# Second MLP's first layer: seven products of halves for eight

## The chip, the cores and the metric

One core of a Trainium2 chip runs the kernel. The metric is the device time of one execution in microseconds (us). TensorE multiplies into PSUM banks; VectorE (DVE), ScalarE (ACT) and GpSimd (POOL) work on tiles in SBUF, and VectorE and ScalarE also read PSUM; the DMA queue of SyncE (SP) moves tiles between SBUF and DRAM.

## The reference

Landmark attention over q, k, v of shape (4, 8, 576, 64) gives 2304 tokens of 512 numbers; a gated MLP with 1536 hidden units follows, and then the second MLP with 2048 hidden units, which the change is about:

```python
def _moe2_ref(x, w_in, w_out, alpha):          # x: 2304 x 512
    h = x @ w_in                               # w_in: 512 x 2048
    g = np.maximum(h, 0.0) + alpha * np.minimum(h, 0.0)
    return (g @ w_out).astype(np.float32)      # w_out: 2048 x 512
```

Weights arrive in float64, all else in float32.

## The kernel before

**Arithmetic.** Every large product is made in three terms. `split` (L113) cuts a float32 tile into a high half (ScalarE casts it to the matmul's type) and a low half (VectorE, or POOL where `lo="pool"`, subtracts), and a product is high x low + low x high + high x high (`TERMS`, L57). So a product of 128 x 512 by 512 x n costs 3 x 4 matmuls of n columns.

**First MLP** (L750 to 808). 96 steps, `at` = 24 b + i, each of 12 matmuls of 288 columns in `layer1` (L638) and 12 in `layer2` (L657), which runs two steps behind. Attention of later batches, the folding of weights (`fold`, `take`, `store_folded`, `take_stored`) and the float64 to float32 conversion of the second MLP's weights (`narrow_w2`, from step 36, one tile in 1.4 steps, stored to DRAM as `w2d`) are placed between the steps by tables of step numbers. Its output is stored to DRAM as `x2d`, one tile for 288 tokens.

**Second MLP** (L812 to 908). Tokens go in blocks of 512 (the last has 256). `load_x2` reads a block of `x2d` and splits it, POOL making the low halves. All 32 weight tiles (16 of `w_in`, 16 of `w_out`) are read from `w2d`, split by `convert_w2` and kept in SBUF, the first from step 56 on, most from step 85. For each block and each of the 16 tiles f of hidden units, `layer3` makes 12 matmuls into one bank (tag `gv`, two banks), two VectorE instructions apply the activation, and `split` makes the halves. `layer4` then adds 3 matmuls of 512 columns for each 128 tokens into that token tile's bank (tags `acc` and `att`, six banks); it runs two f behind (`LAG2`, L901):

```python
        behind2.append((i, f, layer3(xs[i], blocks[i][1], f)))
        if behind:
            catch_up()
        if len(behind2) > LAG2:
            catch_up2()
```

**Order.** The program is written once; a scheduler then orders each engine's instructions when the kernel is built, keeping to what each needs and, where several could go, to the order of writing. On the chip each engine works through its own list in order: an instruction that waits holds up all that stand behind it on its engine. Tiles of a tag share its buffers, and a new tile waits until an old one is read. Tag `ws` has 27 buffers of 128 x 1024 float32, the store for weights of both MLPs.

Of the kernel before, what the change touches and what calls it, by code (L numbers as in the profile page):

```python
# [9 lines left out]
F32 = mybir.dt.float32  # L10
F32R = mybir.dt.float32r
# [4 lines left out]
ALU = mybir.AluOpType  # L16
# [5 lines left out]
def tile_landmark_attention_glu_prelu(  # L22
# [66 lines left out]

    w2d = [dpool.tile([P, NW], F32, name=f"w2d{i}", tag=f"w2d{i}") for i in range(2 * NF2)]  # L90
# [603 lines left out]
    def convert_w2(i):  # L694
        t = rpool.tile([P, NW], F32, tag="st2", name="st2", bufs=2)
        nc.sync.dma_start(out=t, in_=w2d[i])
        split(w2_slot(i), t)
# [6 lines left out]
    nc.vector.tensor_copy(alphaT, pa[:, :NF2])  # L704

# [13 lines left out]
    w2_todo, to_narrow = deque(range(2 * NF2)), deque(range(2 * NF2))  # L719
    narrow_pace = 0.0  # L720
    qpool = rpool = None
# [5 lines left out]
    def catch_up():  # L727
# [8 lines left out]
        for m in range(NK):  # L736
# [4 lines left out]
            if f1 == NF1:  # L741
                to = bpool.tile([P, HB], F32, tag="xs", name="xs", bufs=XS_BUFS)
# [7 lines left out]
    for b in range(B):  # L750
# [5 lines left out]
        for i, (half, f, f0, f1) in enumerate(order):  # L756
# [45 lines left out]
            if qpool is not None and at > FOLD_AT[2][-1]:  # L802
                if at % W2_EVERY == 0:
                    if w2_todo and w2_todo[0] < W2_EARLY:
                        convert_w2(w2_todo.popleft())
                if at >= W2_FROM:
                    if w2_todo:
                        convert_w2(w2_todo.popleft())

    blocks = [(n0, min(512, NT - n0)) for n0 in range(0, NT, 512)]  # L812

    def load_x2(n0, n):
        pool = q2pool if n0 // 512 % 2 else qpool
        xs = pool.tile([P, 2, NK, 512], F32R, tag="x2", name="x2", bufs=1)
        for kk in range(NK):
            xr = qpool.tile([P, 512], F32, tag="xr", name="xr", bufs=2)
            done = 0
            while done < n:  # L820
                bl, o = divmod(n0 + done, HB)
                step = min(n - done, HB - o)
                nc.sync.dma_start(out=xr[:, done : done + step], in_=x2d[bl][:, kk, o : o + step])
                done += step
            split(xs[:, :, kk, :n], xr[:, :n], lo="pool")
        return xs

    def layer3(xs, n, f):
        ps = bank("h", "gv")
        w = w2_in[f].rearrange("p a (k c) -> p a k c", k=NK)  # L830
        i = 0
        for a, e in TERMS:
            for kk in range(NK):
                nc.tensor.matmul(  # L834
                    ps[:, :n], lhsT=w[:, a, kk], rhs=xs[:, e, kk, :n], start=(i == 0), stop=(i == 11)
                )
                i += 1
        g = qpool.tile([P, 512], F32, tag="g2", name="g2", bufs=2)
        gs = bpool.tile([P, 2, 512], F32R, tag="A", name="g2s", bufs=4)
        nc.vector.tensor_scalar(  # L840
            out=g[:, :n], in0=ps[:, :n], scalar1=0.0, scalar2=alphaT[:, f : f + 1],
            op0=ALU.min, op1=ALU.mult,
        )
        nc.vector.scalar_tensor_tensor(  # L844
            out=g[:, :n], in0=ps[:, :n], scalar=0.0, in1=g[:, :n], op0=ALU.max, op1=ALU.add
        )
        split(gs[:, :, :n], g[:, :n])
        return gs

    def layer4(acc, gs, f, t):  # L850
        for i, (a, e) in enumerate(TERMS):
            nc.tensor.matmul(  # L852
                acc,
                lhsT=gs[:, a, P * t : P * t + P],
                rhs=w2_out[f][:, e, :],
                start=(f == 0 and i == 0),
                stop=(f == NF2 - 1 and i == 2),
            )
# [13 lines left out]

    order = [(i, f) for i in range(len(blocks)) for f in range(NF2)]
    xs = {0: load_x2(*blocks[0])}
    accs2, behind2 = {}, deque()
    w2_pace = 0.0

    def catch_up2():
        i, f, gs = behind2.popleft()
        n0, n = blocks[i]  # L880
        if f == 0:
            accs2[i] = [
                bank(f"o{t}", ("acc", "att", "acc")[(2 * i + t // 2) % 3]) for t in range(n // P)
            ]
        for t in range(n // P):
            layer4(accs2[i][t], gs, f, t)
            if f == NF2 - 1:
                store(accs2[i][t], n0 + t * P, t)

    for i, f in order:  # L890
        if i == 0 and f == X2_AT[0]:
            while w2_todo:
                convert_w2(w2_todo.popleft())
            rpool.release()
            q2pool = ctx.enter_context(tc.tile_pool(name="q2pool", bufs=1, reuse_waits="tile"))
        if f == X2_AT[i > 0] and i + 1 < len(blocks):
            xs[i + 1] = load_x2(*blocks[i + 1])
        behind2.append((i, f, layer3(xs[i], blocks[i][1], f)))
        if behind:
            catch_up()  # L900
        if len(behind2) > LAG2:  # L901
            catch_up2()
        w2_pace += W2_STEP
        while w2_todo and w2_pace >= 1:
            w2_pace -= 1
            convert_w2(w2_todo.popleft())
    while behind2:
        catch_up2()
# [30 lines left out]
```

## Time and profile before

| | us |
|---|---|
| median of 3 runs | 900.9 (900.38 to 901.02) |
| profiled execution | 904.5 |
| its span | 902.7 |
| first MLP and attention, until the first matmul of layer 3 | 500.5 |
| second MLP, first to last matmul | 397 |

The profile is of one execution, which took 904.5 us, 1.8 us of it outside the span. Busy time of an engine counts the instructions that compute; TensorE's weight loads (PEld) are a row of their own and run beside its matmuls. A matmul's record is longer than its share of TensorE's time, because matmuls overlap; the time from the start of one group to the start of the next is what a group costs.

### The profile page before, as it was taken

The page shows a single profiled execution, that of the slowest core. Times are in us where ns is not written, and L with a number is a line of the kernel's source. Part 1 is how long each engine was busy: PE and PEld are TensorE (multiplying, and loading weights), DVE is VectorE, ACT ScalarE, POOL GpSimd, SP SyncE. Part 2 cuts the span into 40 slices and gives each one's busy share as a digit, 9 for nine tenths or more (in the row PEclk, how much of TensorE's full clock was granted, in tenths as well). Part 3 has the DMA queues.
Part 4 walks back from the last instruction along what each step waited for, and adds up shares of the span by engine and source line. Part 5 has one row for each costly group of instructions (what it writes and reads, how often), then busy time and mean ns, then how long its engine had stood idle before and what let it go on. Part 6 is the DMA issues. An engine that isn't in the chain of part 4 may idle for free.

```text
span 902.7 us, 15122 instructions
## 1 busy us (share of the span) xinstructions
PE 855.3 (95%) x5969; PEld 712.0 (79%) x5969; DVE 506.6 (56%) x1005; ACT 337.2 (37%) x711; POOL 92.4 (10%) x90
## 2 busy tenths in 40 slices
PE   5689889899999999998999999999999999999997
PEld 4367667676887877998999888888888888888896
DVE  3788988577756344676745654443444433444443
ACT  6666865465654233465535421121121111111111
POOL 0131112110111000134100020110010001000000
PEclk9679999989999999999999999999999999999999
DMA  9676778969612152687824520030012000100100
GB/s 263 229 228 174 252 237 242 274 227 248 185 45 85 48 170 90 221 297 230 258 78 129 145 70 1 4 90 1 1 24 58 1 1 13 48 0 1 29 20 24
DMA packets 85160, 106.92 MB, mean 118 GB/s; under 512 B 35664, under 2 KB 57184, under 8 KB 85088
## 3 DMA queue, kind: packets, MB, share of 16 engines
q1 hardware_dynamic: 81632, 93.36, 34.3%
q0 software_dynamic: 3456, 12.58, 4.5%
q8 instruction: 47, 0.77, 0.4%
q14 instruction: 25, 0.20, 0.1%
HBM read 78.65 MB, written 27.26 MB: 117 GB/s over the span
## 4 chain that ended last, share of the span: by engine, by line
PE 82%; DMA 7%; DVE 4%; ACT 3%; issue 2%; SPq 1%; POOL 1%; DVEq 0%; ACTq 0%
PE h L834 22%; PE o L852 22%; PE gv L638 15%; PE acc L657 13%; PE psf L600 3%; DMA raw<-in_moe_w_in_dram 2%; PE psq L191 2%; DMA raw<-in_moe_w_out_dram 1%; DMA w2d<-n 1%; DVE raw L139 1%; PE psz L403 1%; PE psv L314 1%; DMA tk<-in_k_dram 1%; PE psa L210 1%; PE psc L210 1%
## 5 line engine op out<-in xcount | busy, mean ns | idle before, releaser
L638 PE MATMUL gv<-A,we 128*128 128x288 f32 x1152 | 198.8, 313 | 6.6 <-ACT g L649 4.1
L638 PEld LDWEIGHTS gv<-A,we 128*128 128x128 f32 x1152 | 167.7, 196 | 37.6 <-issue 24.7
L657 PE MATMUL acc<-gs,wconv 128*128 128x288 f32 x1152 | 184.4, 303 | 6.9 <-DVE gs L116 4.7
L834 PE MATMUL h<-x,w 128*128 128x512 f32 (+1 forms) x840 | 183.7, 368 | 0.0
L657 PEld LDWEIGHTS acc<-gs,wconv 128*128 128x128 f32 x1152 | 163.9, 192 | 18.6 <-issue 9.3
L852 PE MATMUL o<-w,g2s 128*128 128x512 f32 x702 | 170.0, 389 | 0.0
L834 PEld LDWEIGHTS h<-x,w 128*128 128x128 f32 x840 | 148.0, 188 | 27.2
L852 PEld LDWEIGHTS o<-w,g2s 128*128 128x128 f32 x702 | 131.0, 188 | 26.6
L115 ACT CAST g2s<-g 128x512 fp32r<-128x512 f32 (+1 forms) x80 | 46.4, 580 | 277.0 <-DVE g L844 277.0
L840 DVE TENSOR_SCALAR g<-h,alphaT 128x512 f32<-128x512 f32 (+1 forms) x80 | 55.8, 697 | 155.7 <-PE h L834 155.7
L116 DVE TENSOR_TENSOR g2s<-g,g2s 128x512 fp32r<-128x512 f32 (+1 forms) x80 | 55.9, 699 | 54.6 <-ACT g2s L115 54.0
L116 DVE TENSOR_TENSOR gs<-g,gs 128x288 fp32r<-128x288 f32 x96 | 52.8, 550 | 25.6 <-ACT gs L115 25.2
L650 DVE TENSOR_TENSOR g<-g,gv 128x288 f32<-128x288 f32 x96 | 43.1, 449 | 39.7 <-PE gv L638 35.9
L649 ACT ACTIVATE g<-gv 128x288 f32<-128x288 f32 x96 | 39.4, 411 | 54.6 <-PE gv L638 53.3
L130 ACT ACTIVATE raw<-raw 128x512 f32<-128x512 f32 x68 | 46.7, 687 | 34.8 <-DMA raw<-in_moe_w_in_dram 17.8
L115 ACT CAST gs<-g 128x288 fp32r<-128x288 f32 x96 | 41.6, 433 | 45.6 <-DVE g L650 45.2
L116 POOL TENSOR_TENSOR x<-xr,x 128x512 fp32r<-128x512 f32 (+1 forms) x20 | 24.2, 1219 | 315.3 <-ACT x L115 313.3
L139 DVE SCALAR_TENSOR_TENSOR raw<-raw 128x512 uint32<-128x512 uint32 x68 | 50.1, 748 | 7.4 <-ACT raw L134 6.3
L844 DVE SCALAR_TENSOR_TENSOR g<-h,g 128x512 f32<-128x512 f32 (+1 forms) x80 | 51.0, 638 | 2.7
L600 PE MATMUL psf<-wgv,m 64*32 64x512 f32 x384 | 42.3, 620 | 0.9 <-DVE wgv L142 0.5
L116 DVE TENSOR_TENSOR we<-psf,we 128x512 fp32r<-128x512 f32 x36 | 23.5, 684 | 13.1 <-ACT we L115 13.1
L142 DVE SCALAR_TENSOR_TENSOR n<-raw 128x512 uint32<-128x512 uint32 x32 | 24.8, 775 | 9.6 <-DMA w2d<-n 9.5
(129 smaller groups left out, 728.2 us busy)
## 6 DMA issues: line engine op xcount, KB each, us to landing
raw<-in_moe_w_out_dram SPq DMA_DIRECT2D x28, 512.0 KB, 5.4
wgv<-wgvd POOLq DMA_DIRECT2D x24, 512.0 KB, 4.9
raw<-in_moe_w_in_dram SPq DMA_DIRECT2D x16, 512.0 KB, 4.8
w2d<-n SPq DMA_DIRECT2D x32, 256.0 KB, 2.8
st<-w2d SPq DMA_DIRECT2D x32, 256.0 KB, 2.7
raw<-in_moe_w_gate_dram SPq DMA_DIRECT2D x24, 256.0 KB, 4.5
raw<-in_moe_w_val_dram SPq DMA_DIRECT2D x24, 256.0 KB, 4.8
wgvd<-wgv SPq DMA_DIRECT2D x12, 512.0 KB, 6.2
```

What stands on the lines that cost most here:

```text
L115: nc.scalar.copy(dst[:, 0, :], src)
L116: (nc.gpsimd if lo == "pool" else nc.vector).tensor_tensor(out=dst[:, 1, :], in0=src, in1=f32(dst[:, 0, :]), op=ALU.subtract)
L130: nc.scalar.activation(w[:, :, 1], w[:, :, 1], AF.Copy, scale=2.0 ** -112)
L139: nc.vector.scalar_tensor_tensor(out=lo, in0=hi, scalar=0x80000000, in1=lo, op0=ALU.bitwise_and, op1=ALU.bitwise_or)
L600: nc.tensor.matmul(pss[j][LM * h : LM * h + LM], lhsT=att[b, j, "M"][d, u], rhs=wgv[c, j][d, u], start=True, stop=True,)
L638: nc.tensor.matmul(ps[:, :HB], lhsT=We[b, c, j][:, a, 256 * i + P * s : 256 * i + P * s + P], rhs=att[b, j, "A"][half][:, e, :], start=(n ...
L650: nc.vector.tensor_tensor(out=g, in0=g, in1=pss[1][:, :HB], op=ALU.mult)
L657: nc.tensor.matmul(acc[m][:, :HB], lhsT=wout_sb[f][:, a, P * m : P * m + P], rhs=gs[:, e, :], start=(f == f0 and n == 0), stop=(f == f1 - ...
L834: nc.tensor.matmul(ps[:, :n], lhsT=w[:, a, kk], rhs=xs[:, e, kk, :n], start=(i == 0), stop=(i == 11))
L840: nc.vector.tensor_scalar(out=g[:, :n], in0=ps[:, :n], scalar1=0.0, scalar2=alphaT[:, f : f + 1], op0=ALU.min, op1=ALU.mult,)
L844: nc.vector.scalar_tensor_tensor(out=g[:, :n], in0=ps[:, :n], scalar=0.0, in1=g[:, :n], op0=ALU.max, op1=ALU.add)
L852: nc.tensor.matmul(acc, lhsT=gs[:, a, P * t : P * t + P], rhs=w2_out[f][:, e, :], start=(f == 0 and i == 0), stop=(f == NF2 - 1 and i == 2),)
```

## The change

The first layer of the second MLP is made by Strassen's scheme (in the form with seven products and shared sums). The hidden tiles 2g and 2g + 1, the contraction's halves (256 each) and two halves of a group of 768 tokens make a 2 x 2 product of blocks: a11, a12, a21, a22 from `w_in`, b11, b12, b21, b22 from x, eight products of blocks, each 6 matmuls of 384 columns. Seven products of sums of blocks take their place, and their results are added up to h11 (tile 2g, first half of the tokens), h12, h21 and h22.

- There are 3 groups of tokens and 8 pairs of hidden tiles, 24 calls of `pair`. A product has its bank (tag `gv`, two of them) until it is read: product 1 by a ScalarE copy, the others by `plus`, a VectorE addition of a bank to a tile (7 in a pair; product 5 is read by two).
- Sums of weights (4 VectorE instructions of 128 x 256) and the halves of all seven left operands are made in `make_w7`, during group 0 only, a pair or two ahead, and stored to DRAM (`w7d`); groups 1 and 2 load them (`load_w7`, four DMAs a pair).
- Sums of x and their halves (14 tiles of 128 x 2 x 384) are made in `make_x7`: for group 0 at steps 74 and 83 of the first MLP, on ScalarE and VectorE; for the others during the last pair of the group before, half of the low parts on POOL. There are 15 buffers for 14 tiles, so a new one waits until a product of the last pair has been made.
- The activation is two Relus on ScalarE and one VectorE scale-and-add (`activated`).
- Layer 4 follows in `catch_up2`, three matmuls at a time, 12 calls a pair, and is no longer held back by a lag. `convert_w2`, `w2_slot` and `load_x2` are gone; `w_out` is split in `make_w2_out`, pair by pair, in group 0.
- The narrowed weights' tile `n2` has one buffer throughout; it had two in the later part of the first MLP.

```diff
-    W2_OWN, W2_RAW = (0, 1), (29, 30, 31)
-    W2_EARLY, W2_EVERY = 4, 2
-    W2_FROM, W2_STEP, X2_AT = 85, 3, (11, 6)
+    NG, HG = 3, 384
+    X2_AT, W2_AT = (74, 83), (88, 91)
+    X2_LOAD, X2_SPLIT = 6, 7
...
-            st = qpool.tile([P, NW], F32, tag="xr", name="st3", bufs=2)
+            st = rpool.tile([P, NW], F32, tag="st3", name="st3", bufs=2)
...
+    ORDER7 = (1, 2, 6, 7, 5, 4, 3)
+    PLACE7 = {1: (0, 0), 2: (0, 1), 6: (1, 0), 5: (1, 1), 7: (2, 0), 3: (2, 1), 4: (3, 0)}
...
+    def make_w7(g):
+        n = ws_tile("n7", (P, 2, NW), F32)
+        for i in range(2):
+            nc.sync.dma_start(out=n[:, i], in_=w2d[2 * (2 * g + i)])
+        a11, a12 = n[:, 0, :256], n[:, 0, 256:]
+        a21, a22 = n[:, 1, :256], n[:, 1, 256:]
+        s = ws_tile("s7", (P, 4, 256), F32)
+        for o, x, y, op in (
+            (1, a21, a22, ALU.add),
+            (0, s[:, 1], a11, ALU.subtract),
+            (2, a11, a21, ALU.subtract),
+            (3, a12, s[:, 0], ALU.subtract),
+        ):
+            nc.vector.tensor_tensor(out=s[:, o], in0=x, in1=y, op=op)
+        w7[g] = [ws_tile("w7") for _ in range(4)]
+        split2(w7[g][0], n[:, 0].rearrange("p (o c) -> p o c", o=2))
+        split2(w7[g][1], s[:, 0:2])
+        split2(w7[g][2], s[:, 2:4])
+        split2(w7[g][3][:, 0:1], n[:, 1:2, 256:])
+        for i in range(4):
+            m = 2 if i < 3 else 1
+            nc.sync.dma_start(out=w7d[g][i][:, :m], in_=f32(w7[g][i][:, :m]))
...
-        t = pool.tile([P, NW], F32, tag="n2", name="n2", bufs=1 if rpool is None else 2)
+        t = pool.tile([P, NW], F32, tag="n2", name="n2", bufs=1)
...
+    def make_x7(i, ops):
+        b11, b12, b21, b22, t2 = (xf[i][n] for n in ((0, 0), (0, 1), (1, 0), (1, 1), "T2"))
...
+            for kk in range(2):
+                t = home([P, 2, HG], F32R, "x7")
+                x7[i, op, kk] = t
+                split(t, src[:, kk], lo="pool" if i > 0 and kk else "dve")
...
+    def product(i, g, op):
+        ps = bank("prod", "gv")
+        place, o = PLACE7[op]
+        w = w7[g][place][:, o].rearrange("p (a k c) -> p a k c", a=2, k=2)
+        n = 0
+        for a, e in TERMS:
+            for kk in range(2):
+                nc.tensor.matmul(
+                    ps[:, :HG], lhsT=w[:, a, kk], rhs=x7[i, op, kk][:, e],
+                    start=(n == 0), stop=(n == 5),
+                )
+                n += 1
+        return ps[:, :HG]
...
+    def activated(h, f):
+        n = half("n", "gs")
+        nc.scalar.activation(n, h, AF.Relu, scale=-1.0)
+        nc.scalar.activation(h, h, AF.Relu)
+        nc.vector.scalar_tensor_tensor(
+            out=h, in0=n, scalar=minus_alpha[:, f : f + 1], in1=h, op0=ALU.mult, op1=ALU.add
+        )
...
+        split(gs, h)
+        return gs
...
+    def pair(i, g):
+        f = 2 * g
+        ps = product(i, g, 1)
+        p1 = half("p1")
+        nc.scalar.copy(p1, ps)
+        h11 = plus(p1, product(i, g, 2), "h11", "gs")
+        ready(i, f, 0, activated(h11, f))
+        catch_up2(1)
+        u2 = plus(p1, product(i, g, 6), "u2")
+        catch_up2(1)
+        u3 = plus(u2, product(i, g, 7), "u3")
+        catch_up2(1)
+        ps = product(i, g, 5)
+        h22 = plus(u3, ps, "h22", "gs")
+        u4 = plus(u2, ps, "u4")
+        ready(i, f + 1, 1, activated(h22, f + 1))
+        catch_up2(2)
+        h21 = plus(u3, product(i, g, 4), "h21", "gs")
+        ready(i, f + 1, 0, activated(h21, f + 1))
+        catch_up2(2)
+        h12 = plus(u4, product(i, g, 3), "h12", "gs")
+        ready(i, f, 1, activated(h12, f))
+        catch_up2(5)
```

The order of instructions on TensorE in the second MLP before, in the second block of tokens (h is layer 3's bank, o0 to o3 the banks of four token tiles, w2 weights, g2s activated halves):

```order
L834 MATMUL h_6845<-x2_6291,w2_6509 128x512 x12
L852 MATMUL o0_6435<-w2_6463,g2s_6797 128x512 x3
L852 MATMUL o1_6436<-w2_6463,g2s_6797 128x512 x3
L852 MATMUL o2_6437<-w2_6463,g2s_6797 128x512 x3
L852 MATMUL o3_6438<-w2_6463,g2s_6797 128x512 x3
```

A layer 4 group uses halves that were made two layer 3 groups earlier.

TensorE in a pair of the last group now, from the start of product 5 (prod_9678); g2s_9648 are the halves of h11, which comes from product 2 of this same pair, three products earlier in the list:

```order
L950 MATMUL prod_9678<-x7_8908,w7_9482 128x384
L950 MATMUL prod_9678<-x7_8911,w7_9482 128x384
L950 MATMUL prod_9678<-x7_8908,w7_9482 128x384
L950 MATMUL prod_9678<-x7_8911,w7_9482 128x384
L950 MATMUL prod_9678<-x7_8908,w7_9482 128x384
L991 MATMUL o0_8960<-w2_7063,g2s_9648 128x512
L991 MATMUL o1_8973<-w2_7063,g2s_9648 128x512
L991 MATMUL o2_8986<-w2_7063,g2s_9648 128x512
L991 MATMUL o0_8960<-w2_7063,g2s_9648 128x512 x2
L991 MATMUL o1_8973<-w2_7063,g2s_9648 128x512 x2
L991 MATMUL o2_8986<-w2_7063,g2s_9648 128x512 x2
L950 MATMUL prod_9678<-x7_8911,w7_9482 128x384
```

Layer 4 on h11 (nine matmuls) stands inside product 5; the layer 4 of h22, h21 and h12 stands between products 1 and 2 of the next pair, 27 matmuls in a row. The order of products is 1, 2, 6, 7, 5, 4, 3.

VectorE in the same pair (u2, u3 and u4 are running sums, g2s and g2r low halves):

```order
L1008 TENSOR_TENSOR u2_9661<-p1_9633,prod_9654 128x384
L964 SCALAR_TENSOR_TENSOR h11_9642<-n_9644,minus_alpha_176,h11_9642 128x384
L1008 TENSOR_TENSOR u3_9673<-u2_9661,prod_9666 128x384
L125 TENSOR_TENSOR g2s_9648<-h11_9642,g2s_9648 128x384
L1008 TENSOR_TENSOR h22_9685<-u3_9673,prod_9678 128x384
L1008 TENSOR_TENSOR u4_9687<-u2_9661,prod_9678 128x384
L1008 TENSOR_TENSOR h21_9709<-u3_9673,prod_9702 128x384
L964 SCALAR_TENSOR_TENSOR h22_9685<-n_9689,minus_alpha_176,h22_9685 128x384
L1008 TENSOR_TENSOR h12_9731<-u4_9687,prod_9724 128x384
L964 SCALAR_TENSOR_TENSOR h21_9709<-n_9711,minus_alpha_176,h21_9709 128x384
L125 TENSOR_TENSOR g2s_9693<-h22_9685,g2s_9693 128x384
L125 TENSOR_TENSOR g2r_9715<-h21_9709,g2r_9715 128x384
```

The addition of h22 and that of u4, both from product 5, stand next to each other; the addition of h12, from product 3, stands behind the scale-and-add of h22. On ScalarE the cast of h22 stands behind both Relus of h21.

VectorE at the same place of a pair in group 0, with the weights of a later pair between (s7 and n7: sums of weights and their sources, w7 the low halves of the left operands):

```order
L707 TENSOR_TENSOR s7_7201<-n7_7198 128x256
L1008 TENSOR_TENSOR h12_7012<-u4_6968,prod_7005 128x384
L707 TENSOR_TENSOR s7_7201<-s7_7201,n7_7198 128x256
L125 TENSOR_TENSOR g2s_6974<-h22_6966,g2s_6974 128x384
L964 SCALAR_TENSOR_TENSOR h21_6990<-n_6992,minus_alpha_176,h21_6990 128x384
L707 TENSOR_TENSOR s7_7201<-n7_7198 128x256
L707 TENSOR_TENSOR s7_7201<-n7_7198,s7_7201 128x256
L689 TENSOR_TENSOR w7_7206<-n7_7198,w7_7206 128x2x256
L125 TENSOR_TENSOR g2r_6996<-h21_6990,g2r_6996 128x384
L964 SCALAR_TENSOR_TENSOR h12_7012<-n_7014,minus_alpha_176,h12_7012 128x384
L689 TENSOR_TENSOR w7_7207<-s7_7201,w7_7207 128x2x256
L689 TENSOR_TENSOR w7_7208<-s7_7201,w7_7208 128x2x256
```

Four sums and three of the four low halves of w7 now stand among the scale-and-adds and the subtractions of h22, h21 and h12.

## Rows read from the trace of the kernel before

**Rows 1.** The page: busy time, share and instructions of each engine.

```profile
PE 855.3 (95%) x5969; PEld 712.0 (79%) x5969; DVE 506.6 (56%) x1005; ACT 337.2 (37%) x711; POOL 92.4 (10%) x90
```

**Rows 2.** By stretch, busy us of PE, PEld, DVE, ACT, POOL; TensorE's clock; DMA.

```profile
500.50:897.50 397.00, 396.89 (x1851) 332.51 (x1849) 175.54 (x264) 67.22 (x119) 18.30 (x16) 1.00 0.10 27
417.00:437.00 20.00, 15.43 (x95) 14.38 (x96) 15.03 (x26) 10.38 (x23) 5.45 (x4) 0.91 0.78 242
```

**Rows 3.** Timeline of TensorE, second MLP: start us, us, engine line op tiles shapes xcount.

```profile
705.23 2.88 PE L834 MATMUL h<-x,w 128*128 128x512 f32 x12
707.95 2.88 PE L852 MATMUL o<-w,g2s 128*128 128x512 f32 x12
...
850.85 1.60 PE L834 MATMUL h<-x,w 128*128 128x256 f32 x12
852.28 2.91 PE L852 MATMUL o<-w2r,g2s 128*128 128x512 f32 x12
```

**Rows 4.** Timeline of TensorE, first MLP near its end.

```profile
475.30 1.75 PE L638 MATMUL gv<-A,we 128*128 128x288 f32 x12
476.89 1.75 PE L657 MATMUL acc<-gs,wconv 128*128 128x288 f32 x12
```

**Rows 5.** Groups by line of weight loads 460:490 (us, mean ns); busy us, 455:500.

```profile
L638 PEld LDWEIGHTS gv<-A,we 128*128 128x128 f32 x116 | 15.9, 188 | 0.0
...
455.00:500.00 45.00, 45.00 (x343) 45.00 (x343) 22.79 (x46) 20.68 (x46) 0.00 (x0) 1.00 0.32 98
```

**Rows 6.** Groups by line, shapes apart: busy us, mean ns | idle before, releaser.

```profile
L844 DVE SCALAR_TENSOR_TENSOR g<-h,g 128x512 f32<-128x512 f32 x64 | 44.2, 691 | 2.1
...
L844 DVE SCALAR_TENSOR_TENSOR g<-h,g 128x256 f32<-128x256 f32 x16 | 6.8, 424 | 0.6
...
L115 ACT CAST g2s<-g 128x512 fp32r<-128x512 f32 x64 | 39.9, 623 | 239.7 <-DVE g L844 239.7
...
L115 ACT CAST g2s<-g 128x256 fp32r<-128x256 f32 x16 | 6.5, 408 | 37.2 <-DVE g L844 37.2
```

**Rows 7.** Timeline of all engines, second MLP, one block's chain.

```profile
702.51 2.65 PE L852 MATMUL o<-w,g2s 128*128 128x512 f32 x11
702.71 0.75 DVE L840 TENSOR_SCALAR g<-h,alphaT 128x512 f32<-128x512 f32 x1 [2.51 <-PE h L834]
...
704.29 0.62 ACT L115 CAST g2s<-g 128x512 fp32r<-128x512 f32 x1 [4.82 <-DVE g L844]
704.95 0.69 DVE L116 TENSOR_TENSOR g2s<-g,g2s 128x512 fp32r<-128x512 f32 x1 [0.77 <-ACT g2s L115]
```

**Rows 8.** Timeline in the first MLP beside POOL; POOL's group of splits.

```profile
398.94 1.75 POOL L116 TENSOR_TENSOR we<-st,we 128x512 fp32r<-128x512 f32 x1
...
399.45 1.54 DVE L116 TENSOR_TENSOR gs<-g,gs 128x288 fp32r<-128x288 f32 x1
...
L116 POOL TENSOR_TENSOR x<-xr,x 128x512 fp32r<-128x512 f32 x16 | 21.3, 1339 | 233.8 <-ACT x L115 231.8 <-DVE n L142 1.9
```

**Rows 9.** Timeline of all engines in the stretch where TensorE waits.

```profile
422.48 1.30 DVE L116 TENSOR_TENSOR gs<-g,gs 128x288 fp32r<-128x288 f32 x1 [2.94 <-ACT gs L115]
...
423.83 1.89 PE L657 MATMUL acc<-gs,wconv 128*128 128x288 f32 x12 [1.59 <-DVE gs L116]
...
425.24 0.44 DVE L650 TENSOR_TENSOR g<-g,gv 128x288 f32<-128x288 f32 x1
...
425.38 2.96 POOL L116 TENSOR_TENSOR x<-xr,x 128x512 fp32r<-128x512 f32 x2 [1.92 <-DVE n L142]
...
425.61 1.62 DVE L139 SCALAR_TENSOR_TENSOR raw<-raw 128x512 uint32<-128x512 uint32 x1
...
427.15 1.52 DVE L116 TENSOR_TENSOR gs<-g,gs 128x288 fp32r<-128x288 f32 x1
...
428.81 0.64 PE L657 MATMUL acc<-gs,wconv 128*128 128x288 f32 x3 [1.49 <-DVE gs L116]
...
430.66 0.67 PE L657 MATMUL acc<-gs,wconv 128*128 128x288 f32 x3 [1.21 <-DVE xs L746]
```

More of the change, by code (lines that the diff above doesn't have):

```diff
@@ L88, in tile_landmark_attention_glu_prelu @@
     }
+    w7d = [
+        [dpool.tile([P, 2, NW], F32, name=f"w7d{g}_{i}", tag=f"w7d{g}_{i}") for i in range(4)]
+        for g in range(NF2 // 2)
+    ]
     w2d = [dpool.tile([P, NW], F32, name=f"w2d{i}", tag=f"w2d{i}") for i in range(2 * NF2)]
@@ new lines, in tile_landmark_attention_glu_prelu, with load_x, room @@
+    x7, xf = {}, {}
+    def load_x(i):
+        def room(first):
+            if i == 0:
+                if first:
+                    t = home([P, 2, HG], F32, "xf")
+                    return t
+                return ws_tile("xf", (P, 2, HG), F32)
+            if first:
+                return wpool.tile([P, 2, HG], F32, tag="raw", name="xf", bufs=4)
+            return ws_tile("xf", (P, 2, HG), F32)
+        bs = {}
+        for j, th in ((0, 0), (0, 1), (1, 1), (1, 0)):
+            t = room(j == 0)
+            at0, done = (2 * i + th) * HG, 0
+            while done < HG:
+                bl, o = divmod(at0 + done, HB)
+                step = min(HG - done, HB - o)
+                nc.sync.dma_start(
+                    out=t[:, :, done : done + step],
+                    in_=x2d[bl][:, 2 * j : 2 * j + 2, o : o + step],
+                )
+                done += step
+            bs[j, th] = t
+        bs["T2"] = room(False)
+        xf[i] = bs
@@ L801, in tile_landmark_attention_glu_prelu @@
                     narrow_pace -= 1
[L802 to L835, printed above, removed]
-                )
[L837 to L858, printed above, removed]
+            if at == X2_AT[0]:
+                load_x(0)
+                make_x7(0, ORDER7[:4])
+            if at == X2_AT[1]:
+                assert not to_narrow
+                rpool.release()
+                q2pool = ctx.enter_context(
+                    tc.tile_pool(name="q2pool", bufs=1, reuse_waits="tile")
+                )
+                make_x7(0, ORDER7[4:])
@@ L871, in store @@
             done += step
[L873 to L906, printed above, removed]
+    def product(i, g, op):
[8 more added lines that the diff above has]
+                    start=(n == 0), stop=(n == 5),
+                )
+                n += 1
+        return ps[:, :HG]
@@ new lines, in tile_landmark_attention_glu_prelu, with ready, catch_up2 @@
+    accs2, count, behind2 = {}, {}, deque()
+    def ready(i, f, th, gs):
+        behind2.extend((i, f, th, t, gs) for t in range(3))
+    def catch_up2(n):
+        for _ in range(min(n, len(behind2))):
+            i, f, th, t, gs = behind2.popleft()
+            u = 3 * th + t
+            if (i, u) not in accs2:
+                accs2[i, u] = bank(f"o{u}", "acc" if (6 * i + u) % 6 < 4 else "att")
+                count[i, u] = 0
+            acc = accs2[i, u]
+            count[i, u] += 1
+            for k, (a, e) in enumerate(TERMS):
+                nc.tensor.matmul(
+                    acc,
+                    lhsT=gs[:, a, P * t : P * t + P],
+                    rhs=w2_out[f][:, e, :],
+                    start=(count[i, u] == 1 and k == 0),
+                    stop=(count[i, u] == NF2 and k == 2),
+                )
+            if count[i, u] == NF2:
+                store(acc, 2 * i * HG + u * P, u)
@@ new lines, in half, with plus @@
+    def half(name, tag="xs"):
+        return bpool.tile(
+            [P, HG], F32, tag=tag, name=name, bufs=XS_BUFS if tag == "xs" else GS_BUFS
+        )
+    def plus(x, ps, name, tag="xs"):
+        c = half(name, tag)
+        nc.vector.tensor_tensor(out=c, in0=x, in1=ps, op=ALU.add)
+        return c
+    def pair(i, g):
[21 more added lines that the diff above has]
+        catch_up2(5)
@@ new lines, in tile_landmark_attention_glu_prelu @@
+    while behind:
+        catch_up()
+    make_w7(1)
+    make_w2_out(1)
+    for i in range(NG):
+        for g in range(NF2 // 2):
+            if i == 0 and 1 <= g and g + 1 < NF2 // 2:
+                make_w7(g + 1)
+                make_w2_out(g + 1)
+            elif i > 0 and g + 1 < NF2 // 2:
+                load_w7(g + 1)
+            elif g + 1 == NF2 // 2 and i + 1 < NG:
+                load_w7(0)
+            if i + 1 < NG and g == X2_LOAD:
+                load_x(i + 1)
+            pair(i, g)
+            if i + 1 < NG and g == X2_SPLIT:
+                make_x7(i + 1, ORDER7)
```

70 lines of the change are left out of this document (52 added, 18 removed).

## The prediction

> **What bounds the kernel now.** The page first: TensorE is busy 95% of the span [rows 1]. The busy time by stretches then says where: in the second MLP, 500.5 to 897.5 us, TensorE is busy 396.9 of 397.0 us at clock 1.00 [rows 2], so nothing but its own work sets the time there; VectorE has 175.5 us of work and ScalarE 67. From 417 to 437 us, in the first MLP, TensorE is busy only 15.4 of 20 us at clock 0.91. The timeline of TensorE gives the price of its work: starts of groups of 12 matmuls. 705.23 to 707.95 is 226.7 ns for a matmul of 512 columns, 850.85 to 852.28 is 119.2 ns for 256 [rows 3], 475.30 to 476.89 is 132.1 ns for 288 [rows 4]. That is columns at 2.4 GHz (213.3, 106.7, 120.0) plus 12 to 13 ns, so **384 columns cost 160 + 12.6 = 172.6 ns**.
>
> **Part 1, the matmuls.** The first layer had 12 x 16 x 4 = 768 matmuls of 512 columns and 12 x 16 = 192 of 256: 768 x 226.7 + 192 x 119.2 = 174.1 + 22.9 = 197.0 us. The order of the changed kernel has 7 x 6 x 24 = 1008 of 384: 1008 x 172.6 = 174.0 us. **-23.0 us**, all on the path. The second layer keeps its 864 matmuls of 512 (195.9 us).
> The time of one weight load speaks against that price: 188 ns [rows 5], more than 172.6. But from 455 to 500 us the weight loads are 100% busy [rows 5], while TensorE starts a matmul every 132.1 ns without idling: loads overlap one another, and the price stands. The Trainium skill (Perfetto Trace Analysis, section Identifying the Most-Contended Engine) judges how near TensorE is to its limit by the busy share of LDWEIGHTS; by that rule the first MLP is at the limit, and the products would go no faster than one load each. The trace shows 132 ns at that share, so I follow the row and keep the rule as a rival.
>
> **Part 2, the waits inside a pair.** Before, a block had one VectorE chain per 24 matmuls and layer 4 lagged two blocks behind. Now each product is read by an addition on VectorE before its bank is free, with two banks, and layer 4 follows its own pair closely. For 384 columns I go midway between the rows for 256 and 512 [rows 6]: VectorE (424 + 691) / 2 = 0.56 us, ScalarE (408 + 623) / 2 = 0.52. An independent VectorE instruction behind another starts 0.37 us after one of 0.44 us (425.24 to 425.61) [rows 9], so 0.47 or 0.48 after one of 0.56. Hand-overs: TensorE to VectorE 0.20 us after the next group's start (702.51 to 702.71 [rows 7]), VectorE to ScalarE 0.11, ScalarE to VectorE 0.04, which I also take from ScalarE to ScalarE [rows 7]; to TensorE 0.05 (422.48 + 1.30 to 423.83) [rows 9].
> TensorE needs 42 x 0.1726 + 36 x 0.2267 = 15.4 us for a pair. VectorE needs 15 x 0.56 = 8.4 and ScalarE 13 x 0.52 = 6.8, so neither is the bound; what counts is when each result is ready. I walk through the order of a pair of the last group:
> - Product 3 takes the bank of product 5, which h22 and u4 both read: 0.20 + 0.47 + 0.56 + 0.05 = 1.28 us after product 5, while TensorE has only product 4, 1.04 us. Wait 0.25.
> - Layer 4 on h11 needs, after product 2: addition, two Relus, scale-and-add, cast = 0.20 + 0.56 + 0.11 + 0.52 + 0.04 + 0.52 + 0.04 + 0.56 + 0.11 + 0.52 + 0.05 = 3.23 us; TensorE has products 6, 7 and five matmuls of 5 in between, 17 x 0.1726 = 2.93. Wait 0.3.
> - Layer 4 on h22 stands one product into the next pair. Its cast stands on ScalarE behind both Relus of h21, and ends 1.06 us after product 3; product 1 takes 1.04. Wait 0.07.
> About 0.6 us a pair, of the 23.0 / 24 = 0.96 it saves. With VectorE and ScalarE at the 256-wide prices the chains take 1.0 and 2.6 us and the waits vanish: bound 0. At the 512-wide prices the first is 0.5, the second 0.9: bound 1.4. I take the middle, as 384 is.
> In six pairs of the first group weights are made as well: on VectorE 4 x 0.42 + 3 x 0.69 + 0.42 + 2 x 0.69 = 5.6 us more, 14 of some 16 us. The order puts seven of these ahead of the halves of h21 and h12, whose subtractions come late by 0.2 and 0.1: 0.9 us a pair. I read no wait on the w7d stores and the loads of the next weights there. **18 x 0.6 + 6 x 0.9 = +16.2 us** (bounds 0 and 24 x 1.4 = 34).
>
> **Part 3, the seams.** *Start*: pair 0 has no layer 4 of an earlier pair between its products; the h11 and h22 chains each show, **+1.0** (0 to 3, an Activation table load among them). *Between groups, twice*: 14 splits of x, ScalarE 14 x 0.52 = 7.3 us, VectorE 3.9 for 7 low halves and 4 x 0.96 for sums of 768 (0.69 and another 0.27), POOL 7 x 1.34 x 384 / 512 = 7.0 [rows 8], beside a pair that is full at 15.4; and the first additions of the new group wait for buffers that the stores of the old one hold. A VectorE subtraction of 288 columns took 1.54 us beside a POOL one [rows 8], over twice the 0.69 of 512 columns alone, so the seven POOL halves may cost it up to 7. Two pairs have 31 - 17 = 14 us free on VectorE, so most hides: I take 3 each, **+6** (2 to 14). *End*: no product is left to cover the last chains. Layer 4 on h22 waits 1.1 us after product 3; the order puts the addition of h12 behind both earlier subtractions and one copy of an output, so that layer 4 on h12 waits 1.7 more: **+2.8** (1 to 5). What follows the last matmul stays.
>
> **Part 4, the first MLP.** The splits of x for group 0 move to steps 74 and 83: VectorE 14 x 0.56 + 4 x 0.96 = 11.7 us, ScalarE 7.3; the conversions of 32 weight tiles that stood there and later (0.69 and 0.62 each) go to the pairs counted above. VectorE has 22.8 of 45 us busy at 455 to 500 [rows 5], so they fit. POOL no longer splits x at 425 us, where two VectorE instructions took 1.62 and 1.52 us and TensorE then waited 1.49 and 1.21 [rows 9]; against that the narrowed weights have one buffer where they had two, and each waits for the write before it. I take **0** (-8, all of the loss at 417 to 437: 4.6 us idle and 0.09 x 20 of clock, rounded up; +8, that loss once more).
>
> **Sum:** -23.0 + 16.2 + 1.0 + 6 + 2.8 + 0 = +3.0. The profiled execution took 904.5 us (span 902.7), 3.6 above the median of the runs, 900.9; I put the sum on the median: **903.9 us**. A difference of 0.2%, 1.8 us, is about what a measurement can tell.
>
> **Rivals.**
> 1. *Faster: the first MLP loses its stall.* Place: 417 to 437 us. If no POOL split of x blocks VectorE there, the two late subtractions that held TensorE [rows 9] come in time. Price: up to 8 us, so 895.9. It decides if TensorE waits less than 1 us in all there. Against: the first of the waits, 1.59 us, is for a subtraction that was already 2.94 us late by ScalarE before the x splits began [rows 9], and POOL keeps the splits of the folded weights.
> 2. *Slower: seams and weights at their upper end.* If each between-groups seam costs 7 and not 3, VectorE being held by POOL, the time is 903.9 + 8 = 911.9. For: the 1.54 us of [rows 8]. Against: VectorE's free time in the two pairs.
> 3. *Slower: the weight path sets the pace.* 1008 x (188 - 172.6) = 15.5 us more, 919.4. Against, nearly conclusive: [rows 4, 5].
> That the change does not do what it says is no rival: the order shows 1008 and 864 matmuls.
>
> **Chances.** Forecast 0.45, with 897 to 911 for its unknown prices; rival 1 0.30, rival 2 0.21, rival 3 0.04. Faster by over 0.2%: rival 1 and 0.06 of the forecast, 0.36. Within: 0.16, all from the forecast. Slower: 0.23 of the forecast and rivals 2 and 3, 0.48. 893 to 914 leaves out rival 3, the far end of rival 2 and the case in which the waits in the pairs vanish. The forecast alone would have 897 to 911.
>
> **What would show it.** Right: 172 to 173 ns between matmuls of 384 columns at clock 1.00; TensorE idle about 0.6 us a pair in the last group, before the last product (VectorE) and before layer 4 on h11 (ScalarE's cast); pairs of 16.0 us there and 16.3 in the first group; a visible gap between groups, with VectorE instructions over 1 us beside POOL. Wrong: 188 ns a matmul (rival 3); TensorE without idle in a pair (part 2 falls, some 888); pairs of the first group over 17 us; or a first MLP that ends more than 4 us earlier or later.

## The result and the profile after

The changed kernel takes **915.5 us** (median of 4; 911.4 to 918.7) where the kernel before took 900.96 beside it: ratio 1.0148 [1.0124, 1.0173]. It is slower, and 915.5 lies above the range of 893 to 914. A second measurement (below) gave 913.4, just inside that range, against 902.4: 1.0126 [1.0096, 1.0156].

The profiled execution took 911.4 us with a span of 909.6. The page's busy times, beside [rows 1], show TensorE's work 3 us less, VectorE's 79 us and ScalarE's 119 us more:

```profile
PE 852.3 (94%) x6017; PEld 711.6 (78%) x6017; DVE 585.6 (64%) x1214; ACT 456.4 (50%) x981; POOL 83.7 (9%) x84
```

The busy times by stretch answer to [rows 2]: the stall of the first MLP, the whole second MLP, and the 50 us around the first change of groups.

```profile
417.00:437.00 20.00, 18.51 (x137) 17.94 (x136) 17.64 (x36) 12.73 (x31) 0.00 (x0) 1.00 0.82 258
495.90:903.40 407.50, 395.30 (x1874) 333.97 (x1872) 245.34 (x443) 185.61 (x382) 15.90 (x14) 1.00 0.39 128
600.00:650.00 50.00, 45.95 (x208) 37.84 (x207) 32.85 (x53) 24.14 (x51) 7.93 (x7) 0.97 0.48 153
```

The second MLP takes 407.5 us, from the first product to 226.7 ns after the start of the last matmul. Before it took 393.4: from 500.7 to 897.2, less 24 matmuls of the first MLP (3.2 us) that still stood inside. Its matmuls alone would take 174.0 + 195.9 = 369.9 us at the prices of the prediction, so **37.6 us are lost, where 26.0 were forecast**. The 12.2 us in which TensorE is not busy are only part of them, because the profile models the ends of matmuls, and these cover short waits; a pair's own length shows the rest.

The timeline of TensorE, two ordinary pairs of the last group (start us, us, engine line op tiles shapes xcount):

```profile
803.59 4.18 PE L950 MATMUL prod<-x,w 128*128 128x384 f32 x23
...
815.89 2.21 PE L991 MATMUL o<-w,g2r 128*128 128x512 f32 x9
817.93 2.20 PE L991 MATMUL o<-w,g2s 128*128 128x512 f32 x9
819.97 4.18 PE L950 MATMUL prod<-x,w 128*128 128x384 f32 x23
824.16 2.31 PE L991 MATMUL o<-w,g2s 128*128 128x512 f32 x9
826.30 3.80 PE L950 MATMUL prod<-x,w 128*128 128x384 f32 x19
...
836.33 0.87 PE L950 MATMUL prod<-x,w 128*128 128x384 f32 x4
```

819.97 - 803.59 = 16.38 and 836.33 - 819.97 = 16.36 us a pair, 0.95 over 15.41, with no idle time printed. The idle time of the weight loads (PEld) shows what TensorE waited for in one pair, 812.6 to 828.9 (waited for: us in total, times, longest):

```profile
PEld prod L950 <- DVE u L1008: 0.4, 1, 0.4
PEld o L991 <- DVE g2s L125: 0.3, 1, 0.3
PEld o L991 <- ACT g2s L124: 0.3, 1, 0.3
```

Those stand where part 2 put its three waits: the last product's bank, layer 4 on h22, layer 4 on h11. They come to 1.0 us of idle weight loads; by the starts of single matmuls they delay TensorE by 0.32 us (380 and 285 ns between starts where 173 and 173 are usual), 0.19 (307 and 337 for 227 and 227) and 0.28 (348 and 333 for 173 and 227), 0.79 together.

The second of them has another cause than the forecast gave. Not ScalarE's cast of h22 was late, which ended at 813.47, before the group's first matmul at 813.62, but VectorE's subtraction for the low half, which the group's fourth matmul needs:

```profile
812.98 0.49 ACT L124 CAST g2s<-h 128x384 fp32r<-128x384 f32 x1
...
813.78 0.55 DVE L125 TENSOR_TENSOR g2s<-h,g2s 128x384 fp32r<-128x384 f32 x1
...
814.39 1.23 PEld L991 LDWEIGHTS o<-w,g2s 128*128 128x128 f32 x6 [0.34 <-DVE g2s L125]
```

At the first change of groups the waits are long enough to be idle time of TensorE itself (600 to 650 us), and VectorE's timeline shows why:

```profile
PE prod L950 <- DVE u L1008: 3.2, 4, 1.6
PE o L991 <- ACT g2r L124: 0.4, 1, 0.4
```

```profile
614.76 1.00 POOL L125 TENSOR_TENSOR x<-xf,x 128x384 fp32r<-128x384 f32 x1 [0.29 <-POOL x L125]
614.81 0.54 DVE L1008 TENSOR_TENSOR u<-p,prod 128x384 f32<-128x384 f32 x1
615.27 1.30 DVE L783 TENSOR_TENSOR xf<-xf 128x768 f32<-128x768 f32 x1
...
615.94 2.77 POOL L125 TENSOR_TENSOR x<-xf,x 128x384 fp32r<-128x384 f32 x2 [0.18 <-ACT x L124]
616.50 1.35 DVE L964 SCALAR_TENSOR_TENSOR h<-n,minus_alpha,h 128x384 f32<-128x384 f32 x1
...
617.77 0.54 DVE L1008 TENSOR_TENSOR u<-u,prod 128x384 f32<-128x384 f32 x1
...
618.37 1.01 PE L950 MATMUL prod<-x,w 128*128 128x384 f32 x2 [1.62 <-DVE u L1008]
```

A sum of x that takes 0.95 us elsewhere takes 1.30, a scale-and-add of 0.62 takes 1.35, both beside POOL; the addition that TensorE waits for stands behind them. By the starts of each pair's first product, pairs 7 and 8 (counted from 0) take 20.19 and 18.97 us, and pairs 14 to 16 take 17.11, 18.95 and 19.00: 6.4 and 6.0 us over ordinary ones.

The first change holds something more. At the end of the wait of 1.62 us TensorE's granted clock fell to 0.50, 1.2 GHz, for 3.4 us; after the same wait at the second change it stayed at 1.00 (stretches as in [rows 2], then TensorE's timeline):

```profile
618.20:621.60 3.40, 3.23 (x8) 2.75 (x9) 3.40 (x8) 1.66 (x4) 0.51 (x1) 0.50 0.72 284
756.00:759.10 3.10, 2.75 (x11) 2.07 (x12) 3.10 (x7) 1.78 (x4) 0.69 (x1) 1.00 0.76 296
```

```profile
619.17 3.38 PE L991 MATMUL o<-w,g2s 128*128 128x512 f32 x9
622.39 2.26 PE L950 MATMUL prod<-x,w 128*128 128x384 f32 x12
...
756.35 0.62 PE L950 MATMUL prod<-x,w 128*128 128x384 f32 x2 [1.62 <-DVE u L1008]
756.80 2.48 PE L991 MATMUL o<-w,g2s 128*128 128x512 f32 x9
759.12 2.27 PE L950 MATMUL prod<-x,w 128*128 128x384 f32 x12
```

The same eleven matmuls take 622.39 - 618.37 = 4.02 us there and 759.12 - 756.35 = 2.77 us here, so 1.25 of the 6.4 us are the lower clock.

### The profile page after: what moved, and what is told of

It reads as the page before. It is cut to its first block, busy times and chain, and to the rows that moved or that the text cites. A ratio compares the mean times of both kernels' runs of the same rounds, so it can differ in the third digit from the quotient of the medians.

```text
span 909.6 us, 15881 instructions
## 1 busy us (share of the span) xinstructions
PE 852.3 (94%) x6017; PEld 711.6 (78%) x6017; DVE 585.6 (64%) x1214; ACT 456.4 (50%) x981; POOL 83.7 (9%) x84
## 4 chain that ended last, share of the span: by engine, by line
PE 76%; DVE 9%; ACT 5%; DMA 5%; issue 3%; POOL 1%; SPq 1%; DVEq 0%; ACTq 0%; POOLq 0%
PE o L991 20%; PE acc L666 15%; PE gv L647 15%; PE prod L950 15%; PE psf L609 3%; PE psq L200 2%; DMA raw<-in_moe_w_in_dram 2%; DVE h L964 1%; PE psc L219 1%; PE psz L412 1%; PE psa L219 1%; DVE raw L148 1%; DVE h L1008 1%; PE psv L323 1%; DMA tk<-in_k_dram 1%
## 5 line engine op out<-in xcount | busy, mean ns | idle before, releaser
L950 PE MATMUL prod<-x,w 128*128 128x384 f32 x1008 | 195.9, 340 | 7.7 <-DVE u L1008 6.7
L950 PEld LDWEIGHTS prod<-x,w 128*128 128x128 f32 x1008 | 176.8, 188 | 22.0 <-DVE u L1008 16.2
L991 PE MATMUL o<-w,g2s 128*128 128x512 f32 x576 | 148.3, 401 | 2.0 <-ACT g2s L124 1.2
L991 PEld LDWEIGHTS o<-w,g2s 128*128 128x128 f32 x576 | 105.2, 189 | 33.2 <-ACT g2s L124 7.2
L962 ACT ACTIVATE n<-h 128x384 f32<-128x384 f32 x96 | 50.4, 525 | 138.5 <-DVE h L1008 138.5
L991 PE MATMUL o<-w,g2r 128*128 128x512 f32 x288 | 74.6, 398 | 2.5 <-ACT g2r L124 1.9
L964 DVE SCALAR_TENSOR_TENSOR h<-n,minus_alpha,h 128x384 f32<-128x384 f32 x96 | 61.7, 643 | 16.2 <-ACT h L963 12.8
L991 PEld LDWEIGHTS o<-w,g2r 128*128 128x128 f32 x288 | 52.2, 188 | 18.1 <-ACT g2r L124 5.3
L1008 DVE TENSOR_TENSOR h<-u,prod 128x384 f32<-128x384 f32 x72 | 39.8, 552 | 34.9 <-PE prod L950 32.3
L963 ACT ACTIVATE h<-h 128x384 f32<-128x384 f32 x96 | 50.4, 525 | 2.6
```

What stands on the lines that cost most here:

```text
L950: nc.tensor.matmul(ps[:, :HG], lhsT=w[:, a, kk], rhs=x7[i, op, kk][:, e], start=(n == 0), stop=(n == 5),)
L962: nc.scalar.activation(n, h, AF.Relu, scale=-1.0)
L963: nc.scalar.activation(h, h, AF.Relu)
L964: nc.vector.scalar_tensor_tensor(out=h, in0=n, scalar=minus_alpha[:, f : f + 1], in1=h, op0=ALU.mult, op1=ALU.add)
L991: nc.tensor.matmul(acc, lhsT=gs[:, a, P * t : P * t + P], rhs=w2_out[f][:, e, :], start=(count[i, u] == 1 and k == 0), stop=(count[i, u] = ...
L1008: nc.vector.tensor_tensor(out=c, in0=x, in1=ps, op=ALU.add)
```

## The experiments

Times are medians of 4 to 6 runs (12 in experiment 4, one in 9); the ratio is to the kernel before on the same chip. "The second MLP" is measured as above, in the profiled execution.

**1. The changed kernel again.**

> The changed kernel once more, unaltered, for a second trace and more times beside the kernel before. Theory A (the second MLP alone makes it slower; the first MLP's stall comes and goes between executions of either kernel): the second MLP, from its first product to its last matmul, takes 407.5 us again to within 1 us, while what stands ahead of it differs by some us from the first trace (495.9 us); median 913 to 917. Theory B (the first half is systematically faster by the 8 us that the two traces show, and the profiled execution of the kernel before was a slow one): what stands ahead of the second MLP is 495.9 again to within 1 us and the time is 911 to 912.

913.4 us, 1.0126 [1.0096, 1.0156]. The second MLP takes 406.8 us, its start lies at 498.2 and not 495.9. Theory A holds. The clock falls again at the first change of groups, and only there.

**2. Layer 4 held back.** `older(n)` takes the place of `catch_up2(n)` and leaves six entries (two halves) waiting; one call after each product:

```diff
+        older(2)
         h11 = plus(p1, product(i, g, 2), "h11", "gs")
...
-        catch_up2(5)
+        older(1)
+    def older(n):
+        catch_up2(min(n, max(0, len(behind2) - 6)))
```

> Layer 4 is held back by two halves, and after each product stand six of its matmuls (three after products 1 and 3 alternate), in place of runs of 27 and 9 that follow their own pair. Theory A (a pair's 0.95 us over its matmuls is waiting: for the casts of halves just made, and for the bank that two additions still read): pairs of the last group take 15.4 to 15.5 us, 24 x 0.9 = 22 us less, and the waits behind the last product (2.3 us) and of the first pair go too: 915.5 - 24 = 891 to 894. Rival (the pair's 0.95 us is the price of changing between 384 and 512 columns, paid at each change of operation): it changes 14 times a pair in place of 4, so pairs get no shorter, and if each change costs 0.24 us the time is 915.5 + 24 x 2.4 = 973.

**888.7 us, 0.9843 [0.9817, 0.9868]**: faster than both kernels. The second MLP takes 380.0 us, an ordinary pair 15.69, and over the whole second MLP TensorE waits this much:

```profile
PE prod L950 <- DVE u L1008: 2.2, 2, 1.1
PE prod L950 <- ACT p L1015: 0.2, 1, 0.2
```

The rival falls: TensorE changes between 384 and 512 columns 14 times a pair and gets faster. 0.28 us a pair is left over 15.41, so pairs are longer than Theory A had them; the time is still below its 891 to 894, because the changes of groups shrank too, to 1.7 and 1.5 us over ordinary pairs with the same work for x beside them.

**3. No POOL in the splits of x.** `lo="dve"` for all of them.

> The low halves of the next group's x that POOL made (7 a group) are made on VectorE. Theory A (the seams cost 6 us each because VectorE is held while POOL works: instructions of 0.55 us took 1.06 and one of 0.62 took 1.35): VectorE has 7 x 0.56 = 3.9 us more of work a seam and some 5 us less of stretching, so each seam gets 1 to 3 us shorter: 909.5 to 913.5. Rival (the seams are a matter of how much work stands there, wherever it is done): each gets 2 to 4 us longer, 919 to 923.

911.0 us, 1.0100 [1.0066, 1.0133]; the second MLP takes 404.0, 2.8 to 3.5 less. The first change of groups costs 3.2 us in place of 6.4, as Theory A says; the second still costs 5.9, with waits of another kind (layer 4 for a cast, 1.3 us). But here the clock fell at the second change (0.50 from 779.9 to 783.3 us) and not at the first: the twelve matmuls after that cast take 4.27 us (779.48 to 783.75), where those of the changed kernel take 2.73 (776.62 to 779.35). Without the lower clock the changes are 5.2 and 6.0 us with POOL and 3.2 and 4.4 without, so both get shorter, by what Theory A allowed (1 to 3 us).

**4. No sums and splits of x for the later groups** (their products read the first group's x).

> The sums, differences and splits of x for the second and third group are left out, and their products read those of the first group (so the work of 14 splits and 4 sums a group is missing; the loads stay). Theory A (this work beside a full pair is what the seams cost): the two seams of 6.4 and 6.0 us over ordinary pairs fall to under 1 us each, 915.5 - 11 = 904 to 906. Rival (the seams are waits of the new group's additions and of layer 4 for buffers and banks that the stores of the old group hold): they keep at least 3 us each, 909 or more.

903.9 us, 1.0029 [1.0008, 1.0050]; the second MLP takes 396.4. The changes of groups cost 0.7 and 1.1 us, about as Theory A says. So 10.6 of the 12.4 us there come with this work, the lower clock included; the small rest holds, at the first change, one wait of 0.65 us for an addition.

**5. Eight plain products in the held-back kernel.** Four banks of twelve matmuls a pair; the sums, differences and the copy of product 1 go:

```diff
-        for a, e in TERMS:
-            for kk in range(2):
+        for j in range(2):
+            w = w7[g][fh][:, j].rearrange("p (a k c) -> p a k c", a=2, k=2)
+            for a, e in TERMS:
+                for kk in range(2):
...
-                    start=(n == 0), stop=(n == 5),
+                        start=(n == 0), stop=(n == 11),
```

> Strassen's products are taken out of the held-back kernel: eight products of plain halves (four banks of twelve matmuls a pair), still 768 tokens a group and weights kept in DRAM, no sums of weights or x and no additions behind the products. Theory A (a matmul less is worth its price on TensorE, and the grouping by 768 costs nothing by itself): a pair has 48 x 0.175 + 36 x 0.231 = 16.7 us where the held-back kernel had 15.69, so the second MLP takes 380.0 + 24 = 404, less up to 3 for the smaller seams: 909 to 913, about 9 above the kernel before. Rival (layer 1 by eight would have run as fast, because the additions cost what the seventh saved): 886 to 892.

909.1 us, 1.0084 [1.0061, 1.0107]. TensorE's timeline:

```profile
783.27 2.27 PE L922 MATMUL prod<-x,w 128*128 128x384 f32 x12
785.38 1.55 PE L963 MATMUL o<-w,g2s 128*128 128x512 f32 x6
...
800.02 2.27 PE L922 MATMUL prod<-x,w 128*128 128x384 f32 x12
```

800.02 - 783.27 = 16.75 us a pair, with TensorE busy throughout. Seven products (15.69) save 1.06 us a pair, 25 us in 24 pairs. Over the whole second MLP it is 401.7 - 380.0 = 21.7 us, and 24.8 when the changes of groups cost nothing (experiments 10 and 11). The grouping by 768 with eight products is dearer than the kernel before (401.7 against 393.4 us).

**6. Held back, but in one run a pair.** All calls of layer 4 behind the last product, nine entries kept.

> Layer 4 is held back by three halves, but in one run of 34 matmuls a pair, so that the products of a pair stand together as in the changed kernel and two matmuls of layer 4 stand ahead of the last. Theory A (two separate waits: 0.5 to 0.6 us a pair for casts, which go here, and 0.32 for the bank that two additions read, of which what is not covered by the two matmuls, 0.46 us, stays): pairs of 15.4 to 15.6, so as good as the held-back kernel: 886 to 891. Rival (only the alternation of products and layer 4 makes the chains on VectorE and ScalarE fit, since seven products in 7.3 us leave the additions no time): the bank waits grow, pairs of 16 or more, 896 to 904.

889.1 us, 0.9869 [0.9844, 0.9894]; pairs of 15.73; one wait of 0.2 us for the bank is left in a pair. The alternation is not what does it.

**7. Spread as in 2, but nothing held back** (6 becomes 0).

> The calls of layer 4 are spread over the products as in the held-back kernel, but nothing is held back, so that layer 4 follows its own pair again. Theory A (what layer 4 waits for is its halves' casts, and holding back is what counts): 0.5 to 0.7 us a pair stays, and the end's waits too: 903 to 909. Rival (the order of calls was all): 886 to 892.

906.7 us, 1.0058 [1.0039, 1.0077]; pairs of 16.27, with the three waits of the changed kernel. Theory A holds: holding back is what counts.

**8. Splits of x issued later, in the held-back kernel.**

```diff
+        if i > 0 and g == 0 and ORDER7.index(op) > 0 and ORDER7.index(op) + 2 < 7:
+            make_x7(i, ORDER7[ORDER7.index(op) + 2 : ORDER7.index(op) + 3])
...
-                make_x7(i + 1, ORDER7)
+                make_x7(i + 1, ORDER7[:3])
```

> The held-back kernel, in which the sums and splits of the next group's x behind the third product are issued inside the new group's first pair, two products ahead of their use, in place of all of them ahead of it. Theory A (what is left of the seams, 1.3 us each, is the new pair's additions standing behind splits in VectorE's order; the waits of 1.1 us for an addition before a product are that): both go, 1 to 2.5 us less than the held-back kernel, 886 to 888. Rival (VectorE simply has more to do than fits beside two pairs while POOL holds it): same time, 888 to 890.

888.8 us, 0.9865 [0.9840, 0.9890]: no change, and the two waits of 1.1 us stay. A miss: they stand in the old group's last pair, behind the first three steps, which this edit leaves where they were.

**9. The kernel before again.**

> The kernel before once more, for a second trace. Theory A (what stands ahead of the second MLP differs between executions of one kernel by some us, and the changed kernel's first half is no faster): the second MLP takes 396.5 us from its first product to its last matmul, as in the first trace (500.7 to 897.2), while its start lies elsewhere by 1 to 5 us, and the stall at 417 to 437 us is shorter or longer. Theory B (the stall belongs to the kernel before): the start is 500.7 to within 1 us.

902.4 us (one run). The second MLP takes 396.9 us of wall time again, but starts at 498.3 and not 500.7; in 417 to 437 us TensorE idles 3.0 us where it idled 4.6. Theory A holds.

**10. Held back, no POOL.**

> The held-back kernel with all low halves of the next group's x on VectorE. Theory A (what is left of the seams, 1.3 us each, is VectorE held by POOL: its instructions there take 0.9 to 1.4 us in place of 0.55): the waits of 1.1 us go, 886 to 888. Rival (it is the amount of work on VectorE beside a full pair): 7 x 0.56 = 3.9 us more a seam, of which up to 2 shows: 889 to 892.

886.6 us, 0.9834 [0.9811, 0.9856]. All ordinary pairs and those at the changes of groups take 15.69 to 15.71 us, the second MLP 376.9, and one wait of 0.3 us is left. Theory A holds.

**11. Held back, two sums of x a pair earlier** (POOL keeps its splits).

```diff
-            if op == 6:
-                sub(b11, b12, b11)
-                sub(t2, b22, b11)
+            if op == 0:
+                sub(t2, b12, b11)
                 sub(b12, b22, b12)
+                continue
+            if op == 6:
+                sub(b11, b22, t2)
...
+            if i + 1 < NG and g == X2_SPLIT - 1:
+                make_x7(i + 1, (0,))
```

> The held-back kernel, with two of the four sums of the next group's x (0.95 us each on VectorE) made a pair earlier, where they wait for no buffer; the differences are formed in another order of the same terms. Theory A (an addition of the old group's last pair stands behind such sums and splits on VectorE, and TensorE waits 1.1 us for it): about that wait goes, 1 us a seam: 886 to 888. Rival (the wait is for splits that stand behind freed buffers, so moving sums changes nothing): 888 to 890.

886.6 us, 0.9845 [0.9819, 0.9872]; the same 376.9 us and no wait at the changes. Either remedy is enough: VectorE was late by little.

**12. As 10, products two at a time** (calls of 0, 4, 0, 4, 0, 4, 0 entries).

> The held-back kernel without POOL's splits, with products two at a time and twelve matmuls of layer 4 between them: TensorE changes between the two kinds 7 times a pair in place of 14. Theory A (the 0.28 us a pair that is left over the matmuls' price is a slower start of each stretch after a change, 20 ns each): pairs of 15.69 become 15.55, 24 x 0.14 = 3.4 us less: 882 to 885. Rival (it belongs to the matmuls of 384 columns wherever they stand): 15.69 stays, 885 to 888. Third (product 1 follows product 3 with one product between, so a wait for a bank comes back): 15.8 or more, 889 or more.

**884.7 us, 0.9814 [0.9785, 0.9842]**, the lowest median. Pairs take 15.64, not 15.55: half as many changes of kind are worth 0.05 us, so most of the 0.28 does not belong to them. The intervals of experiments 2, 10, 11 and 12 overlap, so their medians do not rank them; the second MLP does, with 380.0, 376.9, 376.9 and 376.0 us.

## Why the prediction was wrong

The mechanism was right in the main, and two terms of the sum were too small: the two changes of groups (+6, measured 12.4) and the waits in a pair (0.6 us, measured 0.95).

**Part 1 held.** Seven products are worth what was said. Experiment 5 against 2 gives 1.06 us a pair, where six matmuls of 384 columns at 172.6 ns would be 1.04. The forecast 23.0 is against the kernel before, whose blocks are wider: there the second MLP with all waits gone (experiments 10 and 11) is 393.4 - 376.9 = 16.5 us shorter, close to 23.0 less 24 times the 0.28 us a pair of part 2. The weight path (rival 3) did not set the pace: experiment 5 runs 48 products' and 36 layer-4 matmuls in 16.75 us, where 188 ns a load for the products would make 17.2; a pace of one load for each product, which the prediction drew from the rule of the Trainium skill (Perfetto Trace Analysis, section Identifying the Most-Contended Engine), would have cost 15.5 us, which no trace shows.

**Part 2: right places, a wait too small and a term missing.** The step "About 0.6 us a pair" failed: it is 0.95. The waits stand at the three places named, and cost 0.79 us where 0.62 was forecast. The chain for h11 fits: from product 2 to layer 4 it was put at 3.23 us and took 3.12 (821.04, the start of product 6, to 824.16). The wait on h22 was put at 0.07, for a cast on ScalarE; it is 0.19, for the low half on VectorE. Some 0.1 us of each wait is a restart, which was not forecast: the nine layer-4 matmuls that follow a wait took 824.16 to 826.30 = 2.14 us, nine without one 815.89 to 817.93 = 2.04. Experiment 2 has no such wait in an ordinary pair and is 16.37 - 15.69 = 0.68 us shorter. The other 0.16 in the changed kernel, 0.28 in experiment 2, is a term that the sum did not have: matmuls cost a little more here than their price from long stretches [rows 3, 4]. The weights of group 0 were wrongly charged: its pairs take 16.25 to 16.48 us, like the others, and in experiment 2 both groups take 15.69. Sum over the pairs, the start with them: 22.3 us against 17.2.

**Part 3: the seams were mis-sized, and this is the largest miss.** The "+6" for both changes of groups was 12.4, near the upper bound of 14 (rival 2 had 14 for its case). The argument "Two pairs have 31 - 17 = 14 us free on VectorE, so most hides" failed: an average of free time hides nothing that a given addition waits for, and that addition stood behind sums, splits and POOL. The prediction's own terms for VectorE, 3.9 + 3.8 + up to 7 us, already came to more than the 14. Experiment 4 puts 10.6 us on that work, 1.25 of them the lower clock, which no term had; experiment 2 shows that with this work in place holding layer 4 back cuts the two changes to 3.2 us together, and 10 and 11 that a small relief then ends them. *Start* cost 1.7 us, the ordinary waits of its two pairs included, against 1.0 and twice 0.6; *end* was right: 25.40 us for the last pair with what follows, 21.5 of matmuls and 0.95 of ordinary waits, so 2.9 against 2.8. Two waits make most of it:

```profile
895.32 4.41 PE L991 MATMUL o<-w,g2s 128*128 128x512 f32 x18 [0.77 <-ACT g2s L124]
901.22 2.35 PE L991 MATMUL o<-w,g2r 128*128 128x512 f32 x9 [1.50 <-ACT g2r L124]
```

**Part 4: the 0 stands.** The traces seemed to say otherwise, by the forecast's own sign: the first MLP ends 7.9 us earlier after the change (495.9 us) than before (503.8, its 24 matmuls counted). But that execution of the changed kernel was 4.1 us below the median of its runs, and that of the kernel before 3.6 above. In 12 traces of the changed kernel and its variants the second MLP starts at 495.8 to 503.6 us; less each execution's distance from its own median, it starts at 498.6 to 501.1, mean 499.7. The two traces of the kernel before give 500.2 and 500.3 in the same way. The stall at 417 to 437 us shrank (1.5 us idle and clock 1.00, against 4.6 and 3.0 at 0.91), the way rival 1 said though not below its 1 us, but TensorE waits elsewhere: from 350 to 400 us it is now busy 48.0 of 50 us, before 49.3. The gain is about half a microsecond, less than the spread; the 8 us of rival 1 are not there.

**Altogether**: 26.0 forecast and 37.6 measured, 11.6 more, is the distance from 903.9 to 915.5. Both parts missed to the same side. The range stopped at 914 although the bounds of parts 2 and 3 reached 30 us above their values; they were treated as if they could not miss together. That the parts meet 915.5 to the tenth is luck: the second measurement has 11.0 us between the kernels and not 14.5.

**The cause in one line**: Strassen's product saves 25 us here, and the grouping by 768 (8 us) and layer 4 close behind its own pair together with the splits of x (31) took 39 back; with layer 4 held back by two halves the same products give 888.7, with x relieved too 886.6, and 884.7 with products by twos.

## What to carry to other kernels

When a shorter chain of matmuls is bought with additions between them, price the wait of each consumer before the arithmetic saved: here 25 us saved became 11 to 14 lost, and a queue kept two halves longer turned it into a gain. Put new work where nothing that is waited for stands behind it; an engine's average free time does not hide it. When several terms of a sum rest on the same engine being in time, widen the range for all of them missing together.

## What the hardware showed that was not expected

- A wait costs TensorE more than its length: 0.10 us more for nine matmuls after it, in the rows above.
- The same wait of 1.62 us for VectorE was followed by 3.4 us at the lower clock at the first change of groups and by none at the second, 1.25 us of difference. Both traces of the changed kernel have it at the same change; why only there is open.
- POOL's splits stretch only some of VectorE's instructions: in the rows above those with all operands in SBUF took 1.30 and 1.35 us, while an addition that reads a product from PSUM took 0.54, begun 0.05 us after a POOL one. The Trainium skill (SBUF — State Buffer, section SBUF: two separate sides) says that VectorE and POOL lock a pair of ports against each other, and names instructions with two SBUF inputs; these rows agree.
- Matmuls of layer 4 that follow products in short stretches run slower without any wait: in the held-back kernel six took 1.39 us, 231.7 ns each against 226.7 [rows 3]:

```profile
812.12 1.55 PE L991 MATMUL o<-w,g2s 128*128 128x512 f32 x6
813.51 1.21 PE L950 MATMUL prod<-x,w 128*128 128x384 f32 x6
814.55 1.55 PE L991 MATMUL o<-w,g2r 128*128 128x512 f32 x6
```

  36 of them make 0.18 of the 0.28 us that a pair is left over; why is open.
